# Linear attention and a gated MLP on one core: first weight chunk loaded in one piece ahead of the third pair's keys, values between keys, exp table loaded early

## The chip, the core and the metric

The kernel runs on one core of a Trainium2 chip. The metric is the device time of one execution in microseconds. Before the change the median of three runs is 920.73 us (920.37 to 925.24).

## What is computed

For 8 batches and 8 heads, with sequences of 576 and heads of 64, in fp32:

```python
q_s = exp(q - max(q, -1)); q_s /= sum(q_s, -1) + 1e-9     # softmax over the head dimension
k_s = exp(k - max(k, 2));  k_s /= sum(k_s, 2) + 1e-9      # softmax over the sequence
kv  = einsum('bhsd,bhse->bhde', k_s, v)
x   = einsum('bhsd,bhde->bhse', q_s, kv)                  # -> 4608 tokens x 512
h   = x @ w_in                                            # 512 x 2048
out = (h * clip(h + 3, 0, 6) / 6) @ w_out                 # 2048 x 512
```

## The kernel before, in words

The 4608 tokens go in nine blocks of 512 (`j`), the 2048 hidden columns in sixteen chunks of 128 (`f`). A block's attention works on four pairs of heads (`hp`), two heads of 64 beside each other on the 128 partitions. The MLP of a block is `gemm1` per chunk (12 matmuls into `ph`), the gate (ScalarE L560, VectorE L561), a split of the result into a high and a low part (`g_hi`, `g_lo`, L123 and L124), and `gemm2` (12 matmuls into `po`). Each fp32 product is made of three passes with such split factors. From block 2 on, a scheme of seven products per pair of chunks (`fast_pair`) takes the place of the plain gemms.

The weights arrive as float64, seen as pairs of 32-bit words: one chunk is 128 rows of 8 KB, 1 MB, of which the first half is `w_in` (side 0) and the second `w_out` (side 1). `load_w` (L126) loads a chunk or one side of it into `raw`; `decode` (L134) turns a whole chunk into fp32 and splits it: on ScalarE an Abs (L145) and a scaled copy (L156), on VectorE a clamp (L146), a shift (L148), a merge (L153) and an add (L157, a custom operation), then the split, high part on ScalarE (L123), low part on VectorE for even chunks and on GpSimd for odd ones from the fourth on (L124). All sixteen chunks are decoded while block 0 runs. There is one buffer `m` and two buffers `v`, so decodes follow each other closely.

Block 0 is the opening. `load_first` (L188) issues a pair's keys `kT` on SyncE's queue (L192) and its queries on ScalarE's queue (L193); `load_first_v` (L198) issues its values on SyncE's queue. All of them lie in slots that late weights take over. For a pair, VectorE takes the maxima (L262 keys, L252 queries), ScalarE takes exp of the keys (L263) and of the queries (L254), GpSimd subtracts the maximum (L253) and multiplies by the reciprocal sum (L258), TensorE transposes both (L97, `pe` and `tp`), then makes `kv` (into `pkv`) and `x` (into `px`); VectorE normalizes `kv` (L210 to L213) and makes the low part of `x` (L124, `x_lo`). The tile `three` (a column of 3.0, the bias of the gate) is set by GpSimd at L106.

The program's order is not the order on the engines. A scheduler places each engine's instructions from its own estimate of their times, so that a change of three lines moves many rows in the opening. From the first gemm of block 1 the matmuls are kept in program order (`in_order`). The two programs' orders are the same from about row 230 of TensorE and row 355 of VectorE on, which is some 75 us after block 0 has ended. A DMA holds one of eight completion lanes, over all queues, until it has landed, so a ninth is issued only when the first is there.

The loop at the end of the function (before: L596 to L606) makes the order of the loads: keys and queries of the pairs 0 and 1, side 0 of chunk 0, keys and queries of 2 and 3, four values, side 1 of chunk 0, then the chunks 1 to 5. `decode(0)` needs both sides.

Of the kernel before, what the change touches and what calls it, by code (L numbers as in the profile page):

```python
# [13 lines left out]
AF = mybir.ActivationFunctionType  # L14
# [16 lines left out]
def attention_moe(  # L31
# [27 lines left out]
    nc = tc.nc  # L59

    B, NP, _, S = kT.shape
# [43 lines left out]
    three = const.tile([P, 1], F32, name="three")  # L105
# [5 lines left out]
    def place(f, dt, name):  # L111
        return wp.tile([P, 4 * DM], dt, name=name, tag=f"w{f}")
# [13 lines left out]
    def load_w(f, sides=(0, 1)):  # L126
        if f not in raws:
            raws[f] = place(f, U32, f"raw{f}")
        a, b = 2 * DM * sides[0], 2 * DM * (sides[-1] + 1)
        nc.sync.dma_start(  # L130
            raws[f][:, a:b], w[f].rearrange("p s n -> p (s n)")[:, a:b]
        )
# [56 lines left out]
    def load_first(hp):  # L189
        t = borrow(f"kq{hp}")  # L190
        kt, qt, qT = t[:, 0:S], cut(t, S, NC4, 2, D), t[:, S + TB : S + 2 * TB]
        nc.sync.dma_start(kt, kT[0, hp])  # L192
        nc.scalar.dma_start(qt, q[0, hp])  # L193
        t = borrow(f"kv{hp}")
        vt, ke = cut(t, 0, NCH, 2, D + 1), cut(t, NCH * 2 * (D + 1), NCH, P)
        first[hp] = kt, qt, qT, vt, ke

    def load_first_v(hp):  # L198
        nc.sync.dma_start(first[hp][3], v[0, hp])
# [384 lines left out]
    def store(j, po):  # L584
        for t in range(NTT):
# [7 lines left out]
                nc.scalar.mul(ob, po[t], 1.0 / 6.0)  # L593
            nc.sync.dma_start(out[j * TB + t * P : j * TB + (t + 1) * P, :], ob)

    for hp in range(NP):  # L596
        load_first(hp)
        if hp == 1:
            load_w(0, (0,))
    for hp in range(NP):  # L600
        load_first_v(hp)
    load_w(0, (1,))
    AHEAD = 6
    for f in range(1, AHEAD):
        load_w(f)
# [142 lines left out]
```

## Time and profile before

| | |
|---|---|
| median of three runs | 920.73 us |
| profiled execution, its own time | 919.73 us |
| its span | 917.9 us |
| TensorE busy | 865.8 us, 94% |
| VectorE busy | 627.3 us, 68% |
| ScalarE busy | 456.7 us, 50% |
| GpSimd busy | 148.7 us, 16% |
| DMA moved | 182.04 MB, mean 198 GB/s |
| chain that ended last | TensorE 69%, VectorE 9%, DMA 3%, ScalarE 3% |

The shares are means over stages that differ. The opening runs to about 31 us, where the first `gemm1` starts; the sixteen decodes and block 0 run to about 154 us; then come block 1 with plain gemms, to about 250 us, and seven blocks with the seven products. The profiled execution took 1.8 us more than its span; the median of the runs lies 1.0 us above it.

### The profile page before, as it was taken

The page shows a single profiled execution, that of the slowest core. Times are in us where ns is not written, and L with a number is a line of the kernel's source. Part 1 is how long each engine was busy: PE and PEld are TensorE (multiplying, and loading weights), DVE is VectorE, ACT ScalarE, POOL GpSimd, SP SyncE. Part 2 cuts the span into 40 slices and gives each one's busy share as a digit, 9 for nine tenths or more (in the row PEclk, how much of TensorE's full clock was granted, in tenths as well). Part 3 has the DMA queues.
Part 4 walks back from the last instruction along what each step waited for, and adds up shares of the span by engine and source line. Part 5 has one row for each costly group of instructions (what it writes and reads, how often), then busy time and mean ns, then how long its engine had stood idle before and what let it go on. Part 6 is the DMA issues. An engine that isn't in the chain of part 4 may idle for free.

```text
span 917.9 us, 15286 instructions
## 1 busy us (share of the span) xinstructions
PE 865.8 (94%) x5380; PEld 739.7 (81%) x5380; DVE 627.3 (68%) x1265; ACT 456.7 (50%) x937; POOL 148.7 (16%) x329
## 2 busy tenths in 40 slices
PE   5889989999989999999999999999999999999998
PEld 4567657878778888888878888888889898898887
DVE  5999998989776666766666666767666645444333
ACT  6998544545444444545444444444444444444333
POOL 4021432221222120212021211112121201010000
PEclk9899989999999999999999999999999999999999
DMA  9983422448576667666776667665755565557541
GB/s 362 415 313 101 154 72 92 157 127 276 180 254 199 205 202 258 195 213 201 226 224 195 215 210 250 190 212 169 234 178 171 168 209 166 177 167 225 182 140 46
DMA packets 96986, 182.04 MB, mean 198 GB/s; under 512 B 9744, under 2 KB 24080, under 8 KB 94992
## 3 DMA queue, kind: packets, MB, share of 16 engines
q1 hardware_dynamic: 96336, 180.03, 60.6%
q10 hardware_dynamic: 576, 1.05, 0.3%
q8 instruction: 43, 0.70, 0.3%
q14 instruction: 31, 0.25, 0.1%
HBM read 156.93 MB, written 24.12 MB: 197 GB/s over the span
## 4 chain that ended last, share of the span: by engine, by line
PE 69%; DVE 9%; DMA 3%; ACT 3%; issue 1%; POOL 1%; SPq 0%; POOLq 0%; DVEq 0%; ACTq 0%
PE po L91 34%; PE ph L91 27%; PE pz L91 4%; PE px L91 2%; PE pkv L91 2%; DMA out_dram<-ob 2%; DMA qt<-in_qf_dram 1%; DVE qT_lo L124 1%; DVE x_lo L124 1%; DVE x_hi L124 1%; DVE m L302 1%; ACT qT_hi L123 1%; ACT v L433 1%; POOL swap L284 1%; DVE ob L591 1%
## 5 line engine op out<-in xcount | busy, mean ns | idle before, releaser
L91 PE MATMUL po<-w,w 128*128 128x512 f32 x1008 | 261.4, 394 | 2.5 <-DVE ob L591 2.5
L91 PEld LDWEIGHTS po<-w,w 128*128 128x128 f32 x1008 | 178.2, 189 | 33.0 <-DVE ob L591 4.2
L91 PE MATMUL ph<-w,w 128*128 128x256 f32 x1008 | 140.2, 284 | 16.3 <-DVE second L526 16.2
L91 PE MATMUL ph<-x_lo,w 128*128 128x256 f32 (+1 forms) x800 | 152.1, 304 | 1.8 <-ACT second L525 1.5
L91 PEld LDWEIGHTS ph<-w,w 128*128 128x128 f32 x1008 | 132.1, 190 | 23.8 <-DVE second L526 18.5
L91 PE MATMUL ph<-x_hi,w 128*128 128x256 f32 (+1 forms) x592 | 139.0, 339 | 4.6 <-ACT w L123 3.3
L91 PEld LDWEIGHTS ph<-x_lo,w 128*128 128x128 f32 x800 | 117.0, 189 | 16.1 <-ACT second L525 1.7
L91 PEld LDWEIGHTS ph<-x_hi,w 128*128 128x128 f32 x592 | 93.6, 192 | 20.0 <-ACT w L123 5.4
L123 ACT CAST w<-g 128x512 fp32r<-128x512 f32 x112 | 69.5, 620 | 72.8 <-DVE g L535 39.6
L124 DVE TENSOR_TENSOR w<-g,w 128x512 fp32r<-128x512 f32 x112 | 77.8, 695 | 27.6 <-ACT w L123 26.6
L91 PE MATMUL po<-w 128*128 128x512 f32 x336 | 86.2, 393 | 0.0
L124 DVE TENSOR_TENSOR qT_lo<-m,qT_hi 128x512 fp32r<-128x512 f32 x28 | 25.6, 915 | 80.9 <-ACT qT_hi L123 80.8
L91 PE MATMUL po<-w,g_hi 128*128 128x512 f32 x256 | 69.4, 409 | 4.0 <-ACT g_hi L123 3.8
L91 PEld LDWEIGHTS po<-w 128*128 128x128 f32 x336 | 59.6, 189 | 10.4 <-ACT w L123 0.5
L533 ACT ACTIVATE g<-ph,three 128x256 f32<-128x256 f32 x56 | 26.5, 474 | 71.2 <-PE ph L91 71.2
L91 PEld LDWEIGHTS po<-w,g_hi 128*128 128x128 f32 x256 | 47.5, 193 | 16.4 <-ACT g_hi L123 6.4
L284 POOL COPY swap<-qm 32x16 f32<-32x16 f32 x112 | 35.3, 315 | 138.1 <-DVE qm L292 127.8
L535 DVE SCALAR_TENSOR_TENSOR g<-g,ph 128x256 f32<-128x256 f32 x56 | 23.3, 416 | 45.1 <-ACT g L533 45.0
L526 DVE TENSOR_TENSOR second<-second,ph 128x256 f32<-128x256 f32 x56 | 22.8, 408 | 43.4 <-ACT second L525 43.3
L91 PE MATMUL pz<-x_hi,w 128*128 128x256 f32 x336 | 51.5, 290 | 0.0
L91 PEld LDWEIGHTS pz<-x_hi,w 128*128 128x128 f32 x336 | 46.7, 190 | 4.4
L525 ACT COPY second<-ph 128x256 f32<-128x256 f32 x56 | 20.9, 373 | 54.4 <-PE ph L91 54.4
(121 smaller groups left out, 1287.7 us busy)
## 6 DMA issues: line engine op xcount, KB each, us to landing
w<-wf SPq DMA_DIRECT2D x392, 256.0 KB, 2.9
raw<-in_w_dram SPq DMA_DIRECT2D x15, 1024.0 KB, 15.1
out_dram<-ob SPq DMA_DIRECT2D x36, 256.0 KB, 2.7
vt<-in_v_dram SPq DMA_DIRECT2D x28, 325.0 KB, 4.0
wf<-w SPq DMA_DIRECT2D x16, 512.0 KB, 3.9
kt<-in_kT_dram SPq DMA_DIRECT2D x28, 288.0 KB, 3.0
ke<-in_k_dram SPq DMA_DIRECT2D x24, 320.0 KB, 3.2
qt<-in_qf_dram SPq DMA_DIRECT2D x28, 256.0 KB, 3.0
```

What stands on the lines that cost most here:

```text
L91: nc.tensor.matmul(out, lhsT, rhs, start=start, stop=stop, skip_group_check=goes_on)
L123: nc.scalar.copy(hi, src)
L124: engine.tensor_sub(lo, src, hi.bitcast(F32))
L284: nc.gpsimd.tensor_copy(swap[r : r + QD], stat[o : o + QD])
L302: nc.vector.transpose(qT, qt)
L433: nc.scalar.copy(x[:, TB:], px)
L525: nc.scalar.copy(second[:, HT:], x)
L526: nc.vector.tensor_add(second[:, HT:], second[:, HT:], y)
L533: nc.scalar.activation(a, h, AF.Relu, bias=three, scale=1.0)
L535: nc.vector.scalar_tensor_tensor(a, a, 6.0, h, op0=ALU.min, op1=ALU.mult)
L591: nc.vector.tensor_scalar_mul(ob, po[t], 1.0 / 6.0)
```

## The change

```diff
@@ -593,13 +593,17 @@
+    nc.scalar.activation(three, three, AF.Exp)
+    nc.gpsimd.memset(three, 3.0)
     for hp in range(NP):
         load_first(hp)
         if hp == 1:
-            load_w(0, (0,))
-    for hp in range(NP):
+            load_w(0)
+        if hp > 1:
+            load_first_v(hp - 2)
+    for hp in (2, 3):
         load_first_v(hp)
-    load_w(0, (1,))
     AHEAD = 6
     for f in range(1, AHEAD):
         load_w(f)
```

Chunk 0 is loaded by one DMA of 1 MB, rows of 8 KB, in the place where its first side was; the values of the pairs 0 and 1 are issued behind the keys of 2 and 3. ScalarE takes an exp of the column `three`, which brings the load of its table with it, and GpSimd sets the column to 3.0 again. Nothing else is edited.

SyncE's queue in the opening, where `kq` are keys and queries of a pair, `kv` its values, `raw` a weight chunk. Before:

```order
L192 DMA kq_92<-in_kT_dram 128x576
L192 DMA kq_96<-in_kT_dram 128x576
L130 DMA raw_100<-in_w_dram 128x1024
L192 DMA kq_102<-in_kT_dram 128x576
L192 DMA kq_106<-in_kT_dram 128x576
L199 DMA kv_95<-in_v_dram 128x650
L199 DMA kv_99<-in_v_dram 128x650
L199 DMA kv_105<-in_v_dram 128x650
L199 DMA kv_109<-in_v_dram 128x650
L130 DMA raw_100<-in_w_dram 128x1024
```

and now:

```order
L192 DMA kq_94<-in_kT_dram 128x576
L192 DMA kq_98<-in_kT_dram 128x576
L130 DMA raw_102<-in_w_dram 128x2048
L192 DMA kq_104<-in_kT_dram 128x576
L199 DMA kv_97<-in_v_dram 128x650
L192 DMA kq_109<-in_kT_dram 128x576
L199 DMA kv_101<-in_v_dram 128x650
L199 DMA kv_107<-in_v_dram 128x650
L199 DMA kv_112<-in_v_dram 128x650
```

The whole of chunk 0 stands third; its second half stood tenth. On ScalarE's queue the table load and the small exp now stand between the issue of the first pair's queries and those of the other three.

VectorE in the opening, `raw_100` and `raw_102` being chunk 0, `kq_102`, `kq_106` and `kq_104`, `kq_109` the pairs 2 and 3. Before:

```order
L255 TENSOR_REDUCE qr<-kq_106 128x8
L210 TENSOR_SCALAR rk<-pkv 128x1
L256 TENSOR_SCALAR qr<-qr 128x8
L211 RECIPROCAL rk<-rk 128x1
L257 RECIPROCAL qr<-qr 128x8
L213 SCALAR_TENSOR_TENSOR kv<-pkv,rk,mask 128x128
L146 TENSOR_SCALAR m<-m 128x1024
L148 TENSOR_SCALAR m<-m 128x1024
L210 TENSOR_SCALAR rk<-pkv 128x1
L153 SCALAR_TENSOR_TENSOR v<-raw_100,m 128x1024
```

and now:

```order
L257 RECIPROCAL qr<-qr 128x8
L146 TENSOR_SCALAR m<-m 128x1024
L262 TENSOR_REDUCE km<-kq_104 128x1
L148 TENSOR_SCALAR m<-m 128x1024
L252 TENSOR_REDUCE qm<-kq_109 128x8
L255 TENSOR_REDUCE qr<-kq_104 128x8
L153 SCALAR_TENSOR_TENSOR v<-raw_102,m 128x1024
L262 TENSOR_REDUCE km<-kq_109 128x1
L256 TENSOR_SCALAR qr<-qr 128x8
L210 TENSOR_SCALAR rk<-pkv 128x1
L157 ISA v<-raw_102,v 128x2048
```

The clamp of chunk 0 (L146) has gone from the 24th row, behind all of the softmax work, to the 12th, ahead of the maxima of the third pair's keys. Later in the list the low part of chunk 14 has gone from row 192 to row 176, while the gate product of chunk 15 is row 207 in both.

TensorE ahead of the first `gemm1`. Before:

```order
L91 MATMUL pkv<-kv_109 64x65 x8
L91 MATMUL px<-kq_96,kv 128x512
L91 MATMUL pkv<-kv_109 64x65 x2
L91 MATMUL px<-kq_102,kv 128x512
L91 MATMUL px<-kq_106,kv 128x512
L91 MATMUL ph<-x_hi_310,w_305 128x512
```

and now:

```order
L91 MATMUL px<-kq_98,kv 128x512
L91 MATMUL px<-kq_104,kv 128x512
L91 MATMUL pkv<-kv_112 64x65 x10
L91 MATMUL px<-kq_109,kv 128x512
L91 MATMUL ph<-x_hi_311,w_306 128x512
```

The `kv` of the last pair now stands behind two `px`. `px` and `ph` share two buffers, which a `px` frees when VectorE has made its `x_lo`.

## Rows read from the trace of the kernel before

**Rows 1.** Busy time by stretch: us, busy PE, PEld, DVE, ACT, POOL, clock, DMA share, GB/s

```profile
0.00:20.00 20.00, 9.88 (x66) 7.17 (x67) 10.65 (x25) 12.23 (x20) 9.35 (x18) 1.00 0.92 354
...
80.00:100.00 20.00, 19.72 (x105) 15.21 (x104) 19.97 (x33) 15.16 (x36) 3.10 (x2) 1.00 0.46 144
100.00:120.00 20.00, 16.15 (x86) 11.44 (x84) 18.92 (x33) 10.76 (x17) 9.94 (x14) 1.00 0.40 131
120.00:140.00 20.00, 16.00 (x53) 11.12 (x53) 19.18 (x26) 8.06 (x12) 4.81 (x5) 0.83 0.17 54
...
160.00:180.00 20.00, 20.00 (x106) 16.11 (x105) 17.95 (x39) 9.93 (x19) 3.61 (x7) 1.00 0.54 178
```

**Rows 2.** Chain that ended last, 138 to 155 us: start, us, what

```profile
138.39 1.14 DVE w L124
...
139.58 2.60 PE ph L91 x10
...
153.52 0.64 DVE g_lo L124
...
154.21 2.60 PE po L91 x10
```

**Rows 3.** Timeline of VectorE, 4 to 26 us, the idle time ahead in brackets

```profile
4.45 0.75 DVE L262 TENSOR_REDUCE km<-kq 128x1 f32<-128x576 f32 x1 [4.45 <-DMA kq<-in_kT_dram]
...
7.84 0.69 DVE L255 TENSOR_REDUCE qr<-kq 128x8 f32<-128x512 f32 x1 [0.77 <-ACT kq L254]
8.85 0.69 DVE L252 TENSOR_REDUCE qm<-kq 128x8 f32<-128x512 f32 x1 [0.32 <-DMA kq<-in_q_dram]
...
14.19 0.69 DVE L255 TENSOR_REDUCE qr<-kq 128x8 f32<-128x512 f32 x1 [0.77 <-POOL kq L258]
...
17.28 0.69 DVE L146 TENSOR_SCALAR m<-m 128x1024 f32<-128x1024 f32 x1 [1.65 <-ACT m L145]
...
20.04 0.16 DVE L210 TENSOR_SCALAR rk<-pkv 128x1 f32<-128x1 f32 x1 [1.33 <-PE pkv L91]
...
25.66 1.22 DVE L124 TENSOR_TENSOR w<-v,w 128x1024 fp32r<-128x1024 f32 x1
```

**Rows 4.** Timeline of ScalarE, 4 to 17 us

```profile
4.50 1.28 ACT L263 ACT_TABLE_LOAD   x1 [4.50 <-DMA kq<-in_kT_dram]
5.80 1.50 ACT L263 ACTIVATE kq<-kq,km 128x576 f32<-128x576 f32 x2
7.20 0.61 ACT L254 ACTIVATE kq<-kq 128x512 f32<-128x512 f32 x1
...
16.11 1.14 ACT L145 ACTIVATE m<-raw 128x1024 f32<-128x1024 f32 x1
```

**Rows 5.** DMA queues (q1 SyncE, q10 ScalarE), 4 to 6 us: packets, MB, share

```profile
q1 hardware_dynamic: 168, 0.45, 62.5%
q10 hardware_dynamic: 172, 0.31, 40.8%
```

**Rows 6.** DMA issues between 8.6 and 9 us (chunk 0's second half): us to landing

```profile
raw<-in_w_dram SPq DMA_DIRECT2D x1, 512.0 KB, 6.3
```

**Rows 7.** Timeline of GpSimd and VectorE: operations side by side and apart

```profile
11.11 1.04 POOL L258 TENSOR_TENSOR kq<-kq,qr 128x512 f32<-128x512 f32 x1 [0.46 <-DVE qr L256]
26.79 1.22 DVE L153 SCALAR_TENSOR_TENSOR v<-raw,m 128x1024 uint32<-128x1024 uint32 x1
47.57 2.65 POOL L124 TENSOR_TENSOR w<-v,w 128x1024 fp32r<-128x1024 f32 x1 [30.96 <-ACT w L123]
48.00 3.30 DVE L153 SCALAR_TENSOR_TENSOR v<-raw,m 128x1024 uint32<-128x1024 uint32 x1
```

**Rows 8.** Timeline of TensorE, 30 to 32 us

```profile
30.21 2.05 PE L91 MATMUL px<-kq,kv 128*128 128x512 f32 x2 [3.62 <-DVE kv L213]
31.27 1.42 PE L91 MATMUL ph<-x_hi,w 128*128 128x512 f32 x1
```

## The prediction

> **What bounds the kernel now.** I read the busy time by stretches first, since the shares of the whole span mix stages. TensorE is full from 160 us on (20.00 of 20), and so the later stages take what they take; but in the first 20 us it is busy for 9.88, and between 100 and 140 us for 16.15 and 16.00 of 20, 7.9 us idle in all [rows 1]. VectorE is the other way round: 10.65 of the first 20 us, then 19.97 in 80 to 100 and 18.92 and 19.18 in 100 to 140 [rows 1]. So from the opening to the end of block 0 VectorE sets the pace: it decodes sixteen chunks and makes the gates. The chain of waits says the same: the low part of chunk 14 on VectorE releases a `gemm1`, the low part of a gate at 153.52 releases `gemm2` of chunk 15 at 154.21, and from there TensorE waits for next to nothing [rows 2]. I take 154.21 as the mark: what VectorE gains ahead of it moves the rest of the run, if TensorE can follow.
>
> Then the timeline of VectorE's opening. Between its first instruction at 4.45 and the low part of chunk 0 at 25.66 it is idle 0.77, 0.32, 0.77, 1.65 and 1.33 us, 4.8 us in five pieces [rows 3]. The last two stand around the decode of chunk 0, whose first step, the Abs, starts at 16.11 [rows 4], because the chunk's second half was issued at 8.77 and landed 6.3 us later, at 15.1 [rows 6].
>
> **The exp table.** The load takes 1.28 us, from 4.50 to 5.78, and the first exp starts at 5.80; the keys' maximum that it needs (4.45 + 0.75) is there at 5.20 [rows 3, 4]. Loaded early, that exp can run 0.6 us earlier. But the pair of exps ends at 7.30 and the next, of the queries, starts at 7.20 [rows 4], and neither can move: the second needs the second pair's maximum, on VectorE's queue behind two other reductions, at about 6.5; the third needs GpSimd's subtraction at about 7.0. So I cost the table at nothing: VectorE's reductions cover it, and with the cover gone it would be worth 0.6 us. Against it stands the issue of the queries of the pairs 1 to 3, which now waits behind load and exp, 1.3 to 1.5 us. The packets of both queues go out one for one (168 to 172) [rows 5], so the second pair's queries queue behind the first's anyway; if they did come late, the cost is at most the same 0.6 us. I take 0, with ends of minus and plus 0.6. GpSimd's second memset waits for that exp to about 3 us, and its next work comes only with the first queries' maximum near 6.
>
> **Chunk 0 in one piece.** Ahead of its end now lie keys of two pairs (0.59 MB), queries of three (0.79) and itself (1.05): 2.4 MB. By 8 us some 2.0 MB have moved at the rate of rows 5 (0.76 MB in 2 us there, less before and after), so that it lands at about 9.3 in place of 15.1. What is passed pays: the keys of pair 2 come at about 10.7 and those of pair 3 at 12.2, 1 to 2 us later. On VectorE's new list the former are wanted by its 13th row and the latter by its 18th, behind the clamp (about 10.9 us) and the merge (about 14); both are covered. The values of pair 0 move by one place and land near 11.5; `kv` of pair 0 is wanted later than that, near 12.
>
> The Abs then runs at 9.3 to 10.5, and VectorE has the clamp at about 10.9. Walking down its new list with each row's duration, I find the first two gaps again (0.77 and 0.3, waits for the exps of the queries) and none behind them to the low part of chunk 0. So of the 4.8 us, 0.77 + 1.65 + 1.33 = 3.75 go.
>
> **What comes in: GpSimd.** Five of its eight softmax operations of 1.04 us fall between 10.7 and 20 us, and the decode of chunk 0, which stood behind the last of them, now runs beside them. The merge L153 took 1.22 us alone and 3.30 when a GpSimd operation of 2.65 us ran: it ended 1.1 us behind that operation's end [rows 7]. One collision here costs between nothing and 1.04 us. Four operations of the decode are open to it (L146, L148, L153, L157). GpSimd is busy 5.2 of those 9.3 us, and an arrival in the midst waits half an operation: 4 x 0.56 x 0.52 = 1.2 us. The ends are 0 and 4.2 us; I take 1.2, since reductions stand between the four and spread them.
>
> The Trainium skill (page SBUF — State Buffer, section Who interferes with whom) says that a VectorE operation with two SBUF inputs or in a two-port mode and a GpSimd operation that reads SBUF take a shared pair of ports as an exclusive lock for the whole instruction. By that rule the four could each wait a whole operation, 4.2 us, which would eat the gain; the 3.30 us of rows 7 agree with a lock.
>
> **The rest of block 0.** Chunk 14's low part is earlier in VectorE's new list, row 176 for 192, but the gate of chunk 15, which the mark needs, is row 207 in both: the same work lies ahead of it. The seven splits on GpSimd come in the same number and hold VectorE as before. So I carry the head start to the mark unchanged, neither grown nor shrunk, at 3.75 - 1.2 = 2.55, rounded 2.6 us. After the mark I cost the changed order at nothing: TensorE is full and VectorE has 2 us of idle in 20 [rows 1], in which what it put off is done. Were that cover gone, block 1 would wait for a gate.
>
> **The sum.** The profiled execution took 919.73 us; less 2.6 it is 917.1. The median of the runs is 1.0 us above that execution, so for a median I forecast **918.1 us**, 0.3% faster. About 0.5% (4.6 us) is what a measurement here can tell from no change.
>
> **The rivals.** *More: TensorE takes up its idle time.* With weights ready sooner (row 176), the gemms of block 0 could fill part of the 7.9 us between 100 and 140, where also the granted clock was 0.83 [rows 1]. Half of it beside the head start gives 6.5 us: 914.2. For it speaks that TensorE waits for weights there [rows 2]; against it, the unchanged row 207.
>
> *Nothing: the ports eat it.* If the four operations each wait a whole GpSimd operation, the gain is 3.75 - 4.2: 921.2. Rows 7 show such a wait, but behind an operation of 2.65 us.
>
> *Slower: TensorE starts late.* The first `gemm1` starts at 31.27, behind a `px` that waited for `kv` [rows 8]. In the new order the last `kv` stands behind two `px`, and these share two buffers that VectorE frees by `x_lo`, now behind the decode of two more chunks. By the new list the first `gemm1` starts near 33 us, 1.8 later, and 1.2 more with the collisions. TensorE's work from there to the mark is about the same, so it decides whether its waits there shrink by as much. If they stay what they are, the run is 1.8 to 3.0 us slower, 923.2; if VectorE's gates then also come late behind decodes, the double, 926. It speaks against this that TensorE's idle time is there to be used.
>
> **The chances.** The forecast 0.47, more 0.29, nothing 0.13, slower by a late TensorE 0.11. The forecast's own range, by the bounds of the collisions, is 916 to 920. Of "more" about nine tenths lie beyond 4.6 us, and a few parts in a hundred of the forecast: faster 0.30. Of the last, about half lie beyond 4.6 us: slower 0.06. The rest, 0.64, is within 0.5%. For 8 in 10 the range takes in most of "more" and the ports: 912.5 to 922.5.
>
> **What would show it.** Right: the Abs of chunk 0 near 9.3 us; the low part of chunk 0 near 20 to 21; VectorE's idle in the first 25 us down by some 3.7; one to three of the four decode operations of chunk 0 longer than alone; the first `gemm1` near 33 to 34; `gemm2` of chunk 15 near 151.6; every stretch from 300 us on as long as before. Wrong: a chunk 0 that lands after 12 us; a low part of chunk 0 later than 24; idle time of VectorE or TensorE that comes back between 40 and 150 us, above all in waits for gates; a stage behind block 1 that changes, which nothing here would explain.

## The result, and the profile after

The changed kernel takes 915.11 us, the median of six runs (913.89 to 916.72); the kernel before, in the same sets, 920.57 us (919.37 to 925.24, six runs). The ratio is 0.9929, with a 95% interval of 0.9904 to 0.9955: 0.7% faster. The forecast was 918.1 us and "within 0.5%" as the likeliest outcome; the result lies inside the range and nearer to the rival *More* (914.2).

One thing has to be kept apart from the start. The profiled execution of the changed kernel is the slowest of its six, 916.72 us (span 914.7), while that of the kernel before was a quick one, 919.73 us. So the two traces that are compared here differ by 3.0 us, and the medians by 5.5 us. What is said about places is read from the traces; the size is that of the medians.

The page's busy times of the changed kernel are those of before to within 2 us on each engine:

```profile
PE 863.9 (94%) x5380; PEld 740.6 (81%) x5380; DVE 629.0 (69%) x1265; ACT 456.1 (50%) x938; POOL 147.2 (16%) x330
```

So the difference lies in where the engines wait. The opening first. VectorE's timeline of the changed kernel, from 4 to 22 us, as in [rows 3]:

```profile
4.27 0.75 DVE L262 TENSOR_REDUCE km<-kq 128x1 f32<-128x576 f32 x1 [4.27 <-DMA kq<-in_kT_dram]
...
7.69 0.69 DVE L255 TENSOR_REDUCE qr<-kq 128x8 f32<-128x512 f32 x1 [0.77 <-ACT kq L254]
...
10.21 0.69 DVE L252 TENSOR_REDUCE qm<-kq 128x8 f32<-128x512 f32 x1 [0.18 <-DMA kq<-in_q_dram]
...
11.09 1.48 DVE L146 TENSOR_SCALAR m<-m 128x1024 f32<-128x1024 f32 x1
...
13.15 0.86 DVE L148 TENSOR_SCALAR m<-m 128x1024 uint32<-128x1024 uint32 x1
...
15.13 1.69 DVE L153 SCALAR_TENSOR_TENSOR v<-raw,m 128x1024 uint32<-128x1024 uint32 x1
...
17.54 1.21 DVE L157 CUSTOM_DVE_ANT_0 v<-raw,v 128x2048 uint16<-128x2048 uint16 x1
...
19.93 1.79 DVE L124 TENSOR_TENSOR w<-v,w 128x1024 fp32r<-128x1024 f32 x1
...
21.97 1.20 DVE L146 TENSOR_SCALAR m<-m 128x1024 f32<-128x1024 f32 x1
```

Of the five idle pieces two are left, 0.77 and 0.18 us, so 3.9 us of idle time are gone, and the low part of chunk 0 starts at 19.93 in place of 25.66 [rows 3]. In the durations the price can be seen: the clamp L146 takes 1.48 where 0.69 is its time alone, the merge L153 1.69 for 1.22, the low part 1.79 for 1.22. Beside them GpSimd works, in its timeline:

```profile
11.98 1.49 POOL L258 TENSOR_TENSOR kq<-kq,qr 128x512 f32<-128x512 f32 x1
...
19.60 3.02 POOL L258 TENSOR_TENSOR kq<-kq,qr 128x512 f32<-128x512 f32 x2 [3.86 <-DVE qr L256]
```

ScalarE's opening, to be held against [rows 4]; ACTq is its queue of DMA issues:

```profile
1.19 1.28 ACT L597 ACT_TABLE_LOAD   x1 [1.19 <-PEq L734]
1.25 1.35 ACTq L193 DMA_DIRECT2D kq<-in_q_dram  x3
...
9.91 1.14 ACT L145 ACTIVATE m<-raw 128x1024 f32<-128x1024 f32 x1 [1.10 <-DMA raw<-in_w_dram]
```

The Abs waits for the chunk and starts at 9.91, where it was 16.11. The table load is out of the way at 2.47, and the three issues of queries ran beside it, not behind it.

TensorE's timeline, the rows that answer to [rows 8] and the first two of `gemm2` of chunk 15:

```profile
33.84 2.05 PE L91 MATMUL px<-kq,kv 128*128 128x512 f32 x2 [4.47 <-DVE kv L213]
34.90 1.42 PE L91 MATMUL ph<-x_hi,w 128*128 128x512 f32 x1
...
148.42 0.73 PE L91 MATMUL po<-w,g_hi 128*128 128x512 f32 x2 [1.74 <-ACT g_hi L123]
149.15 0.50 PE L91 MATMUL po<-w,g_lo 128*128 128x512 f32 x1
```

and the latter two in the kernel before:

```profile
153.25 0.73 PE L91 MATMUL po<-w,g_hi 128*128 128x512 f32 x2
154.21 0.50 PE L91 MATMUL po<-w,g_lo 128*128 128x512 f32 x1 [0.23 <-DVE g_lo L124]
```

The prediction's mark, 154.21, is the first matmul that takes the low part of the gate; its like is now at 149.15. So the first `gemm1` comes 3.6 us later than before (34.90 for 31.27), and yet the mark comes 5.1 us earlier. The end of block 0 says the same: VectorE's first `ob`, the output that goes to the store, starts at 150.38 for 155.44. TensorE made up 8.7 us in between. Its busy time from the first `gemm1` to that `ob`, before and now (columns as in [rows 1]), shows how:

```profile
31.27:155.44 124.17, 112.58 (x525) 84.00 (x524) 119.12 (x169) 83.59 (x167) 31.46 (x32) 0.95 0.48 176
34.90:150.38 115.48, 108.86 (x525) 82.82 (x524) 113.10 (x164) 80.61 (x163) 29.96 (x32) 0.98 0.49 174
```

It is idle for 6.6 us where it was 11.6, and 525 matmuls, as many as before, keep it busy for 108.9 us where it was 112.6, at a mean granted clock of 0.98 for 0.95. Stretches of 20 us show where:

```profile
100.00:120.00 20.00, 19.82 (x103) 15.19 (x104) 20.00 (x31) 13.11 (x21) 6.22 (x6) 1.00 0.41 128
120.00:140.00 20.00, 17.83 (x88) 12.27 (x87) 19.36 (x30) 8.72 (x14) 8.96 (x12) 1.00 0.52 159
140.00:160.00 20.00, 17.88 (x75) 13.75 (x75) 15.26 (x34) 6.89 (x12) 3.79 (x13) 1.00 0.23 85
160.00:180.00 20.00, 19.77 (x120) 15.82 (x119) 16.65 (x38) 9.83 (x19) 3.88 (x10) 1.00 0.46 147
180.00:200.00 20.00, 18.61 (x78) 14.70 (x77) 16.88 (x36) 7.95 (x17) 5.08 (x12) 0.91 0.36 114
```

Between 100 and 140 TensorE is idle for 2.35 us, where it was 7.85: 5.5 us taken up; the granted clock is 1.00 there, where it was 0.83 from 120 to 140 [rows 1]. But from 140 to 200 it is now idle for 3.7 us (1.74 of them right ahead of `gemm2` of chunk 15), and the granted clock falls to 0.91 in the last stretch, where before TensorE was full from 160 to 200 at 1.00. VectorE's timeline, the rows with a wait for a DMA in that part, shows what is late:

```profile
153.29 0.69 DVE L591 TENSOR_SCALAR ob<-po 128x512 f32<-128x512 f32 x1 [2.22 <-DMA out_dram<-ob]
155.28 0.43 DVE L461 TENSOR_TENSOR ob<-m 128x256 f32<-128x256 f32 x1 [1.30 <-DMA out_dram<-ob]
...
168.41 0.69 DVE L292 TENSOR_REDUCE qm<-qt 128x16 f32<-128x512 f32 x1 [2.79 <-DMA qt<-in_qf_dram]
...
184.94 0.69 DVE L292 TENSOR_REDUCE qm<-qt 128x16 f32<-128x512 f32 x1 [1.51 <-DMA qt<-in_qf_dram]
```

Four waits, 7.8 us: twice for a store that must leave one of the two `ob` buffers, twice for queries of a later block. In the chain of waits the last of them leads, by way of the softmax on VectorE and GpSimd, to a `px` at 188.22, and the `gemm2` behind it starts at a lower clock, granted 0.61 in the mean of its stretch (1.00 is the level of 2.4 GHz, 0.50 that of 1.2), after TensorE was busy for 1.11 of the 2.5 us from 186 on: 4.34 us where the next one takes 2.80:

```profile
180.73 4.19 DMA qt<-in_qf_dram
...
188.22 0.44 PE px L91
188.67 4.34 PE po L91 x12
...
195.92 2.80 PE po L91 x12
```

So the trace has three steps: 5.1 us ahead at the mark, 3.2 at the store that ends block 1 (VectorE's first `ob` of it at 253.89, before at 257.11), and 3.1 at the last one (911.08, before 914.21). From the first `ob` of block 0 to that of block 1 it takes 103.5 us, 1.8 more than before; 1.6 of these are busy time of TensorE, at a mean granted clock of 0.98 for 1.00.

### The profile page after: what moved, and what is told of

It is laid out like the page before. It is cut to its first block, busy times and chain, and to the rows that moved or that the text cites. A ratio compares the mean times of both kernels' runs of the same rounds, so it can differ in the third digit from the quotient of the medians.

```text
span 914.7 us, 15285 instructions
## 1 busy us (share of the span) xinstructions
PE 863.9 (94%) x5380; PEld 740.6 (81%) x5380; DVE 629.0 (69%) x1265; ACT 456.1 (50%) x938; POOL 147.2 (16%) x330
## 4 chain that ended last, share of the span: by engine, by line
PE 66%; DVE 10%; DMA 5%; ACT 2%; issue 1%; POOL 1%; SPq 0%; DVEq 0%; ACTq 0%; POOLq 0%
PE po L91 32%; PE ph L91 25%; PE pz L91 4%; DMA out_dram<-ob 3%; DMA qt<-in_qf_dram 2%; PE px L91 2%; PE pkv L91 2%; DVE m L302 1%; DVE x_lo L124 1%; DVE qT_lo L124 1%; DVE x_hi L124 1%; POOL swap L284 1%; ACT qT_hi L123 1%; DVE ob L591 1%; ACT v L433 1%
## 5 line engine op out<-in xcount | busy, mean ns | idle before, releaser
L124 DVE TENSOR_TENSOR qT_lo<-m,qT_hi 128x512 fp32r<-128x512 f32 x28 | 23.5, 839 | 80.8 <-ACT qT_hi L123 80.8
```

The costliest lines, as they stand in the source:

```text
L124: engine.tensor_sub(lo, src, hi.bitcast(F32))
```

## Experiments

Two theories at first. **T1**: the gain is the head start that the early chunk 0 gives VectorE. **T2**: the gain is another order of the engines' work, which the scheduler happens to make of the new loads. As a third part there is the table load.

**The changed kernel again** (no edit).

> The changed kernel once more, to see how firm its time is and to have a second trace of it. The theory (VectorE's idle time in the opening goes, and the head start reaches the end) expects 915 us again, gemm2 of chunk 15 near 148.4 us in its trace as in the first one, and that the 2 to 3 us which the first trace lost again in block 1 (two loads of queries, 2.8 and 1.5 us waited for, and a stretch of lower clock) are not there or smaller. The rival (block 1 always gives that much back, and the median's larger gain is chance) expects 917 us.

Measured: 915.97 us, ratio 0.9941 [0.9924, 0.9957]. In its trace the gate product of chunk 15 starts at 146.35 (147.03 in the first trace), the first `ob` of block 0 at 150.25 (150.38), the store that ends block 1 at 255.7 (253.9), the last at 911.9 (911.1). The lead at the mark comes back. So do the waits in block 1 (2.20 us for a store, 3.67 and 1.68 for queries), against the expectation that they would be gone or smaller; how much of the lead block 1 gives back varies by 2 us from one execution to the next. Medians of a kernel, measured again, moved by about 1 us: 915.11 and 915.97 here, and 920.57, 920.82, 919.78 and 919.94 for the kernel before.

**Without the table load:**

```diff
-    nc.scalar.activation(three, three, AF.Exp)
-    nc.gpsimd.memset(three, 3.0)
```

> The changed kernel without the early exp and the second memset; TensorE's and VectorE's rows stand in the same order as with them. The theory, that the table load is covered, expects the same time within 1 us, the first exp 0.6 us later and the exp of the first queries at 7.0 to 7.2 us as before. The rival, that the load in front of the keys' exp is on the path, expects 0.6 to 1.3 us more.

Measured: 917.08 us, 0.9951 [0.9933, 0.9968]; TensorE's and VectorE's order is that of the changed kernel, row by row. 1.1 us slower than the repeat, with intervals that overlap; in the trace the first `ob` of block 0 is 0.8 us earlier (149.42 for 150.25).

**The table load alone**, on the kernel before:

```diff
+    nc.scalar.activation(three, three, AF.Exp)
+    nc.gpsimd.memset(three, 3.0)
     for hp in range(NP):
         load_first(hp)
```

> The kernel before with the early exp alone, its order on TensorE and VectorE unchanged. Covered: 920.6 us, no change within 1 us. On the path: 919.3 to 920.

Measured: 917.97 us, 0.997 [0.9957, 0.9984], with the order of the kernel before. By the medians 2.9 us, more than either case expected; by the trace much less: the first `gemm1` at 30.93 for 31.27, the gate of chunk 15 at 151.2 for 151.9. What block 0 shows is 0.3 to 0.7 us.

**The early chunk alone**, with the values behind all keys as they were:

```diff
         if hp == 1:
-            load_w(0, (0,))
+            load_w(0)
     for hp in range(NP):
         load_first_v(hp)
-    load_w(0, (1,))
```

> The kernel before with chunk 0 in one piece ahead of the third pair's keys and nothing else; the values stay behind all keys. If the early chunk is what pays, the time is 915 to 917 us and VectorE is idle some 1 to 2 us of the opening. If the places of the values matter too, the first kv comes 1 to 2 us later and the time is 917 to 919. If the gain came from a lucky order of the rows in block 0, which differs here again, it can be anything from 914 to 922, while the opening still shows the idle time gone.

Measured: 912.17 us, 0.9907 [0.9889, 0.9924]. By the medians this part does more by itself than the whole change, and it lies below all three cases expected. Its gate of chunk 15 is at 143.0, higher up in VectorE's list, but block 0 ends about when it does in the change: the first `ob` is at 149.74 (150.38 there). The store that ends block 1 is at 250.8 and the last at 909.2; against the kernel before that is a lead of 5.7 us at the end of block 0 and 6.3 at the end of block 1, so nothing is given back in block 1. The scheduler made another order of it: in the traces 263 of TensorE's 5380 instructions and 247 of VectorE's 1265 are not what stands at the same place in the changed kernel. The values' place was now the suspect, either by itself or by the order that came with it.

**The values' place alone**, with the chunk in two parts as before:

```diff
     for hp in range(NP):
         load_first(hp)
         if hp == 1:
             load_w(0, (0,))
-    for hp in range(NP):
+        if hp > 1:
+            load_first_v(hp - 2)
+    for hp in (2, 3):
         load_first_v(hp)
     load_w(0, (1,))
```

> The kernel before with one part of the change alone: the values of pair 0 move ahead of the keys of pair 3 (the loop with the values interleaved); the first chunk still comes in two parts, the second of them last; no table load. Theory A (what the change brings is the early first chunk; the values' place is worth nothing either way): within 1 us of before, 919 to 921.5. Theory B (the values among the keys cost VectorE's opening something, by another order of the engines' work or by collisions): slower, 922 to 926, which would fit that the first chunk alone gave 4 us more than the whole change. Theory C (any new order of the planner moves the time by a few us, and the sign is luck): outside 919 to 921.5 on the fast side, 914 to 918.

Measured: 915.82 us, 0.9957 [0.9942, 0.9972]. The chunk comes late, as VectorE's timeline shows:

```profile
16.82 0.69 DVE L146 TENSOR_SCALAR m<-m 128x1024 f32<-128x1024 f32 x1 [1.71 <-ACT m L145]
...
25.97 1.21 DVE L124 TENSOR_TENSOR w<-v,w 128x1024 fp32r<-128x1024 f32 x1
```

VectorE's opening is no better than before (the low part at 25.97), and the median is as good as that of the whole change. By the trace, in this order TensorE's first `gemm1` comes 2.3 us earlier than before (28.97 for 31.27), and that lead is still 2.3 at the end of block 1 (254.83); the other 2.5 of its lead at the last store come behind block 1, where all the kernels run the same instructions in the same order. So an early chunk isn't needed for a gain of some us. Theory C of the expectation, that the order alone moves the time by some us, has a case.

**The early chunk and the table load:** the edit of the early chunk alone, and the two lines of the table load.

> The whole first chunk ahead of the third pair's keys, the values behind all keys (the run with the first chunk alone), and the early exp added; the order of work on TensorE and VectorE is that of the run with the first chunk alone. If the early exp is worth what it showed in the trace of block 0 (0.4 to 0.7 us): 911.0 to 912.0, a ratio to before near 0.990. If it is worth what the timing of the kernel before with it gave (some 2.7 us): 909 to 910.5. If the early chunk already covers it: 912 to 913. With the change's own values' place the time would be 915 to 916, so anything under 914 says that the values' place costs the change some 3 us or more.

Measured: 914.64 us, 0.9933 [0.9909, 0.9956]. By the medians it is 2.5 us slower than without the table load; by the trace, with the same order on both engines, the gate of chunk 15 is 0.1 us earlier and the last store 0.7 us (908.5 for 909.2). None of the three cases that were expected of it fits. The three pairs with and without the table load come out at 2.9 and 1.1 us faster and 2.5 us slower: what the load is worth is under what these medians can tell.

**The early chunk behind the third pair's keys:**

```diff
-        if hp == 1:
-            load_w(0, (0,))
+        if hp == 2:
+            load_w(0)
     for hp in range(NP):
         load_first_v(hp)
-    load_w(0, (1,))
```

> The first chunk whole, but behind the third pair's keys, values behind all keys, no table. The chunk should land some 0.8 to 1.6 us later than in the run with it ahead of them (10.5 to 11.5 where that run has 9.9). If the gain comes from VectorE's opening (idle time gone): still 1.5 to 3 us of it, so that the low part of chunk 0 ends by 21 and the time is 914 to 918. If the gain hangs on the order that the planner makes of block 0: the time can lie anywhere from 911 to 921 with the opening as early; gemm2 of chunk 15 then tells, by the trace, how far block 0 came out ahead (148.4 in the change, 154.2 before).

Measured: 918.67 us, 0.9981 [0.9965, 0.9996]. The Abs starts at 10.82 and the low part of chunk 0 at 20.3, as early as in the change, yet the gate of chunk 15 is at 150.7 (147.0 there, 151.9 before) and the end of block 1 at 257.2 (257.1 before). An early opening isn't enough for a gain of that size either.

**The same, and the values of pair 0 ahead of the fourth pair's keys:**

```diff
         if hp == 2:
             load_w(0)
+            load_first_v(0)
-    for hp in range(NP):
+    for hp in (1, 2, 3):
         load_first_v(hp)
```

> The same as the run with the first chunk behind the third pair's keys, with the values of pair 0 ahead of the fourth pair's keys, as the change has them. TensorE's order of work is the same as in that run, row by row, and VectorE's but for a handful of rows ahead of 25 us: the two differ by the values' place in the queue and by next to nothing else. If the values' place costs by the data's arrival or by collisions: slower than that run by 2 to 4 us. If the values' place costs only by the order that the planner makes of it: the same as that run within 1 us.

Measured: 918.51 us, 0.9981 [0.9965, 0.9996]; 0.2 us from the run before it. With TensorE's order kept, the values' place is worth nothing that the medians show, and the stores that end block 1 are 0.2 us apart (256.99 and 257.23).

What was left to do was to take order and loads apart. In the last four kernels the loads are those of one kernel and the order of work that of another. Behind the traced program stands

```diff
+    for engine, shifts in ORDER.items():
+        mine = [i for i in traced if str(i.engine).split(".")[-1] == engine]
+        row = [mine[k + int(s)] for k, s in enumerate(shifts.split())]
+        for a, b in zip(row, row[1:]):
+            tc.add_manual_dep(b, a.name, dep, reason="order")
```

where `ORDER` lists the other kernel's first 560 rows of TensorE, 370 of VectorE, 240 of ScalarE and 90 of GpSimd, and an edge says only that one instruction is issued behind another. DMA issues are left to the scheduler. The lists of all four engines then agree with the other kernel's from end to end.

**Loads of the kernel before, order of the changed kernel.**

> The loads of the kernel before (first chunk in two parts, the second behind the values; no table load) with the changed kernel's order of work on TensorE, VectorE, ScalarE and GpSimd pinned row by row through block 0. If the time goes with the data: VectorE waits again for the second part of chunk 0 (it lands at 15.1), some 4 us in the opening, now at the head of an order that has nothing else to put there, and the time is 919.5 to 923. If the time goes with the order and the opening's idle time is made up: 915 to 918, gemm2 of chunk 15 within 2 us of the 148.4 of the changed kernel.

Measured: 922.32 us, 1.0038 [1.0026, 1.005]. VectorE's timeline:

```profile
16.22 0.69 DVE L146 TENSOR_SCALAR m<-m 128x1024 f32<-128x1024 f32 x1 [5.32 <-ACT m L145]
...
24.09 1.79 DVE L124 TENSOR_TENSOR w<-v,w 128x1024 fp32r<-128x1024 f32 x1
```

and the same rows of the changed kernel without its table load, where order and loads belong together:

```profile
10.77 0.64 DVE L146 TENSOR_SCALAR m<-m 128x1024 f32<-128x1024 f32 x1
...
18.95 1.79 DVE L124 TENSOR_TENSOR w<-v,w 128x1024 fp32r<-128x1024 f32 x1
```

The clamp stands twelfth in this order and now waits 5.32 us for the chunk, with nothing else to do. The low part is 5.1 us late (24.09 for 18.95), the gate of chunk 15 is 5.1 late (151.2 for 146.1), the end of block 1 is 5.1 late (259.2 for 254.1) and the last store 5.4 (917.5 for 912.1). The waits of block 1 are there all the same, though block 0 ends only 1.0 us earlier than in the kernel before (first `ob` at 154.49):

```profile
157.37 0.69 DVE L591 TENSOR_SCALAR ob<-po 128x512 f32<-128x512 f32 x1 [2.19 <-DMA out_dram<-ob]
...
173.40 0.69 DVE L292 TENSOR_REDUCE qm<-qt 128x16 f32<-128x512 f32 x1 [3.66 <-DMA qt<-in_qf_dram]
```

So they belong to this order, and not to an early start.

**Loads of the changed kernel (without the table load), order of the kernel before.**

> The loads of the changed kernel (first chunk whole ahead of the third pair's keys, values of pair 0 ahead of the fourth pair's keys; no table load) with the order of work of the kernel before pinned row by row through block 0. If the time goes with the data (my prediction's sum: 3.75 us of idle time go from the opening, 1.2 come back by collisions, the rest of block 0 carries the head start): 917 to 918.5, gemm2 of chunk 15 near 151.6 and chunk 0's low part near 21. If the time goes with the order: 919.5 to 921, with the head start gone by chunk 15, at 153.5 to 154.5.

Measured: 920.11 us, 1.001 [0.9988, 1.0033]: no change. ScalarE's timeline and VectorE's:

```profile
15.96 0.59 ACT L271 COPY kv<-pe 128x512 f32<-128x512 f32 x1 [0.94 <-PE pe L97]
...
16.60 1.15 ACT L145 ACTIVATE m<-raw 128x1024 f32<-128x1024 f32 x1
```

```profile
17.79 0.69 DVE L146 TENSOR_SCALAR m<-m 128x1024 f32<-128x1024 f32 x1 [1.42 <-ACT m L145]
...
25.07 1.23 DVE L124 TENSOR_TENSOR w<-v,w 128x1024 fp32r<-128x1024 f32 x1
```

The chunk's DMA takes 7.6 us from issue to landing here (8.2 in the change), but the Abs stands behind the exps of all four pairs and some of their copies and starts at 16.60 without waiting for any data. Chunk 0 lies there and is not used. The low part gains 0.6 us, and 0.1 of it are left at the gate of chunk 15.

**Loads of the kernel before, order of the run with the early chunk alone.**

> The loads of the kernel before with the order of work that the planner made for the run with the first chunk alone early (912.2). If the time goes with the order: 912 to 915. If the early chunk is needed too: the opening's 4 us of idle time come on top, 916 to 919. If the order alone is worth nothing: 919.5 or more.

Measured: 918.14 us, 0.9982 [0.9969, 0.9995]. This order waits 5.32 us at the clamp as well, and is still 1.8 us faster than the old order with the same loads. Against the changed kernel's order, with the same loads and measured beside it (922.32), it is 4.2 us faster, and the intervals do not meet. The traces show where: the first `ob` of block 0 are 0.4 us apart (154.84 here, 154.49 there), the stores that end block 1 are 4.1 (255.15 and 259.21).

**Loads of the changed kernel (without the table load), order of the run with the early chunk alone.**

> The loads of the changed kernel without its table load, with the order of work of the run with the first chunk alone early (912.2): against that run only the values of pair 0 change places with the keys of pair 3. If the values' place costs nothing by itself and the change lost 3 to 4 us through the order that the planner made of it: 911.5 to 913.5. If the values among the keys cost it by the data (keys later, collisions): 915 to 917, as in the change.

Measured: 913.88 us, 0.9947 [0.9935, 0.9959]. Against the run above, which has the same order, was measured beside it and has the loads of before (918.14), it is 4.3 us faster, and the intervals do not meet: that is the early chunk within one order. Against the changed kernel without its table load (917.08) the loads are the same and the order is not; the medians, from two sets of runs, are 3.2 us apart, but the ratios to the kernel before of the same set, 0.9947 and 0.9951, are not. The traces do differ. VectorE's timeline shows how, behind the mark:

```profile
148.84 0.68 DVE L591 TENSOR_SCALAR ob<-po 128x512 f32<-128x512 f32 x1
...
151.78 0.69 DVE L591 TENSOR_SCALAR ob<-po 128x512 f32<-128x512 f32 x1
...
168.05 0.69 DVE L292 TENSOR_REDUCE qm<-qt 128x16 f32<-128x512 f32 x1
```

and the busy time of TensorE (first column) stays whole:

```profile
140.00:160.00 20.00, 20.00 (x104) 15.92 (x103) 17.66 (x36) 8.97 (x15) 3.81 (x13) 1.00 0.30 101
...
180.00:200.00 20.00, 20.00 (x106) 16.14 (x105) 17.80 (x38) 9.04 (x18) 5.83 (x12) 1.00 0.37 114
```

Between the two `ob` four operations of softmax and split stand in this order, done while the first store leaves; in the change the two are neighbours, and VectorE waits 2.22 us there. The load of the queries is issued when VectorE has transposed the last ones (L302); in the change their maximum (L292) is the fourth row behind that, and here the seventh; for the next queries it is the seventh and the twelfth. The store that ends block 1 is at 249.2 here and at 254.1 in the changed kernel without its table load, although their stores of block 0 are 0.6 us apart (148.8 and 149.4).

The medians in one table, loads by order, with the ratio to the kernel before of the same set:

| loads \ order | before | the change | early chunk alone |
|---|---|---|---|
| before | 919.8 to 920.8 | 922.32 (1.0038) | 918.14 (0.9982) |
| the change, no table load | 920.11 (1.001) | 917.08 (0.9951) | 913.88 (0.9947) |
| early chunk alone | | | 912.17 (0.9907) |

The difference between the last two numbers of the right column is the place of the values of pair 0 at one order: 1.7 us by the medians, and more by the ratios, with 912.17 the better, and 1.1 us the other way by the spans of the profiled runs (912.8 and 911.7). It stays open which is better, and whether the values' place is worth anything by itself.

The traces say more than the medians. Times in us by the order of work, over all traces of that order (three, four and four):

| order | first `gemm1`, chunk 0 late | first `gemm1`, chunk 0 early | from it to the first `ob` of block 0 | from that to the first `ob` of block 1 |
|---|---|---|---|---|
| before | 31.27, 30.93 | 30.23 | 123.9 to 125.1 | 100.7 to 102.3 |
| the change | 39.06 | 33.91 to 34.90 | 115.4 to 116.1 | 103.5 to 105.4 |
| early chunk alone | 39.02 | 33.89 to 34.62 | 114.2 to 115.8 | 100.3 to 101.1 |

The two new orders take 8 to 11 us off TensorE's way through block 0, with a late chunk as with an early one, but start it late; the early chunk takes 4 to 5 us off that late start. The change's order then loses some 3 us in block 1.

## Why the prediction was right in part, and where it was wrong

**Right: the opening.** Idle time to the low part of chunk 0 fell by 3.9 us, forecast 3.7; the Abs came at 9.91, forecast 9.3; the low part at 19.93, forecast 20 to 21. The four decode operations cost 0.8, 0.2, 0.5 and 0 us beside GpSimd, 1.5 us together, forecast 1.2. In the two other traces of this order with the early chunk the clamp is not stretched (0.64), and the four cost 0.8 us; so 1.2 lies between, and the exact figure is chance. Two more operations that I had not counted paid 0.6 and 0.5, the low part of chunk 0 and the clamp of the next chunk. The Trainium skill (page SBUF — State Buffer, section Who interferes with whom) describes an exclusive lock for the length of an instruction, by which all four could have met a whole operation, 4.2 us. The traces agree that operations are stretched, and 0.8 to 1.5 us is what this order met.

**Not settled, and one step wrong: the exp table.** Its term was 0, with ends of 0.6. With the load the first `ob` of block 0 comes 0.7 us earlier on the kernel before, 0.1 earlier with the early chunk alone, and 0.8 and 1.0 later in the two traces of the change; the medians disagree too. The step that failed is the issue of the queries, which did not wait behind load and exp. The three issues ended at 2.60, exactly when four issues did before (0.74 + 1.86).

**Wrong: "I carry the head start to the mark unchanged, neither grown nor shrunk".** The mark came 5.1 us earlier, not 2.6. I had looked at the row of the gate of chunk 15, 207 in both, and concluded that nothing else changes. But the rows ahead of it stand in another order, with the weights of late chunks sooner (the rival *More*), and TensorE took up 5.5 us of its 7.85 us of idle time between 100 and 140. Pinning the order tells what is what. Within the changed kernel's order the early chunk's head start does carry unchanged, 5.1 us at each mark down to block 1's end; within the order of the early chunk alone it is 4.2 us at the low part and 5.9 at block 1's end. So the step is nearly true of the loads. It is not true of a new order, which is worth something of its own: with the loads of before, the changed kernel's order ends block 0 1.0 us earlier and costs 2.4 us in the median, and that of the early chunk alone gains 1.8. Why TensorE's way through block 0 is shorter in both is shown only as less idle time and less busy time; that late chunks' weights come sooner is the likely reason, not a tested one.

**Wrong: "After the mark I cost the changed order at nothing".** I had read TensorE as full from 160 us on; it was so to 220, but from 240 to 260 it was busy for 18.02 of 20. And the cover that I named, VectorE's 2 us of idle in 20, was gone: in the changed order VectorE waits 7.8 us for stores and queries between 150 and 185 (1.6 for a store before), TensorE goes idle and loses some clock, and 1.8 of the 5.1 us were given back in the trace, 1.8 to 3.8 over the four traces of this order. My sentence "Were that cover gone, block 1 would wait for a gate" had the right mechanism at no price, though the waits are for stores and queries and not for a gate.

The two errors have opposite signs, which is why the sum was nearly right for the trace: forecast 917.1, measured 916.72. That is luck. For the median it was 3.0 us off, since I set the median 1.0 us above the profiled execution, as it was before, and for the changed kernel it lies 1.6 below.

*Nothing* fell with the collisions. *Slower* had its first step right and more (the first `gemm1` 3.6 us late, forecast 1.8 to 3.0), but its condition did not hold: TensorE's way from there to the mark became 8.7 us shorter. *More* is what happened at the mark, and block 1 then took part of it away.

So the change is faster by an early chunk together with an order that puts its decode into the opening's gaps. Of these two, the early chunk in the old order is worth nothing (920.11), and the new order without the early chunk is a loss (922.32). What the values' move does by itself stays open, but the scheduler answers it with an order that loses some 3 us or more in block 1. The version with the early chunk alone has the lowest median, 912.17 us; with the table load added and the same order it was 914.64, so how far it is ahead of the change is not settled.

## What to carry to other kernels

Where a scheduler places the instructions, an edit of the loads is two changes, the data's arrival and the order, and the profile of before can price only the first; pin one of the two to measure the other. Data that comes early is worth nothing while its first use stands behind other work in the queue, so look for the row that would use it before you count its gain. And read the new order behind the mark too: where it brings together operations that share a pair of buffers, or leaves few rows between the one that frees a buffer and the one that needs what is loaded into it, the stage waits there, whether it starts sooner or not.

## What the runs showed of the hardware

A table load on ScalarE (1.28 us) and DMA issues on the same engine's queue run beside each other: three issues from 1.25 on, 1.35 us in all, with a load from 1.19 to 2.47.

Where VectorE's clamp and a GpSimd operation met in the opening, the one that started second was stretched, and which that was changed from one execution to the next. In the first trace of the changed kernel GpSimd starts at 10.98 and takes 1.04, and the clamp, from 11.09, takes 1.48; in the repeat it is the other way round:

```profile
11.03 0.64 DVE L146 TENSOR_SCALAR m<-m 128x1024 f32<-128x1024 f32 x1
11.08 1.49 POOL L253 TENSOR_TENSOR kq<-kq,qm 128x512 f32<-128x512 f32 x1 [0.69 <-DVE qm L252]
```

Repeated medians of one kernel moved by about 1 us, and two kernels with one order on TensorE and VectorE stood 2.5 us apart by the medians and 0.7 us the other way round by the last store of their traces; a gain under 2 us could be read here only from the times of marks in the traces, and only up to block 1's end: from there to the last `ob`, the same work in the same order, the fourteen traces took 654.6 to 658.9 us.
